# Lightning attention and a gated feed-forward on one core: k and v of two batches held with their chunks in swapped rows, and states made per chunk beside scores and outputs

## The chip, the core and the metric

The kernel runs on one core of a Trainium2 chip. A core has a matrix engine (TensorE, PE in the profile; its weight loads are PEld), a vector engine (VectorE, DVE), a scalar engine (ScalarE, ACT), GpSimd (POOL) and a sync engine (SP). They run side by side, each through its own instructions in order, and wait for each other by semaphores. Matmuls write to PSUM, which has eight banks of 128 partitions by 512 float32; all else lies in SBUF. Loads that change the type from float32 to bfloat16 are issued by GpSimd here, the others by SyncE and ScalarE.

The metric is the device time of one execution in microseconds (us). The kernel before takes 224.22 us, the median of three runs from 223.85 to 224.42.

## What is computed

q, k and v have the shape 4 batches x 8 heads x 768 positions x 64. Attention is linear, with a decay lam per head and causal in blocks of 64; its output goes through a gated feed-forward with 512 inputs, 1536 hidden units and 512 outputs.

```python
for b in range(nb):                                   # blocks of 64 positions
    qb, kb, vb = q[:, :, sl], k[:, :, sl], v[:, :, sl]
    intra = einsum('bhic,bhjc->bhij', qb, kb) * Dmask  # lam ** (i - j) for i >= j
    intra = einsum('bhij,bhjd->bhid', intra, vb)
    inter = einsum('bhid,bhde->bhie', qb * lam_pow, kv_state)
    out[:, :, sl] = intra + inter
    kv_state = lam_block * kv_state + einsum('bhsd,bhse->bhde', kb * rev_pow, vb)
x = out as (batch x position, head x 64)
gate = 1 / (1 + exp(-(x @ w_gate)))
y = (gate * (x @ w_val)) @ w_out
```

## The kernel before

It works in six steps n = 0 to 5 of 128 positions of all four batches, which is 512 rows of the feed-forward. From step 2 on, each step is two chunks c = 0, 1 of 64 positions, and position 64 c + i lies in partition row 64 c + i of the tiles of k and v. `bp` numbers the pairs of batches (0 and 1; 2 and 3).

While TensorE does the feed-forward of step n, it does the attention of step n + 1 in between. The feed-forward is 12 pieces `gv(n, ft)` (four matmuls of 128x512 for the gate `gp`, four for the value `vp`), then four `po(n, tt)` of 12 matmuls each. The list `more[ft]` is put behind piece ft. So TensorE leaves the wide matmuls three times per step, for a burst of small ones of 64x64: the scores (`chunk_s`, behind piece 4, for step 2 behind piece 5), the state products (`chunk_c`, behind piece 8) and the outputs (`chunk_i` and `chunk_a`, behind piece 11).

A matmul of 64x64 uses one quarter of the array: the half of its rows in which its two operands lie, and the half of its columns that is the half of the partitions where its output lies. The loops are laid so that four such matmuls in a row use the four quarters.

Of the eight PSUM banks five go round in `ps_at` (attention) and three in `ps_ff` (feed-forward). A tile of a pool takes the buffer that was given out longest ago, and its first matmul waits until that buffer's last reader is done.

```python
    ps_at = ctx.enter_context(tc.tile_pool(name="ps_at", bufs=5, space=bass.MemoryType.PSUM))
    ps_ff = ctx.enter_context(tc.tile_pool(name="ps_ff", bufs=3, space=bass.MemoryType.PSUM))
    # ...
    def rows_of(u):
        return slice(u * 64, (u + 1) * 64)

    def half(b, h):
        return (1 - h % 2) if b >= NB2 else h % 2

    def load(n, what, b0=0, b1=B):
        sl = slice(n * C, (n + 1) * C)
        for c in what:
            if (c, n) not in T_:
                T_[c, n] = qkv.tile([128, B, H, D], BF16, tag=c + "b", name=c + "b",
                                      bufs=5 if c == "v" else 4)
            src = {"q": q, "k": k, "v": v}[c]
            nat = b1 if n == 0 or c == "v" else min(b1, NB2)
            if b0 < nat:
                nc.gpsimd.dma_start(
                    out=T_[c, n][:, b0:nat],
                    in_=src[b0:nat, :, sl, :].rearrange("b h s d -> s (b h) d"))
            if nat < b1:
                m = max(nat, b0)
                for u in range(2):
                    nc.gpsimd.dma_start(
                        out=T_[c, n][:, m:b1, u::2, :],
                        in_=src[m:b1, 1 - u::2, sl, :].rearrange("b h s d -> s (b h) d"))
    # ...
    def chunk(c):
        return slice(c * L, (c + 1) * L)

    def chunk_s(n, bp):
        sp = [ps_at.tile([128, 2, HP, L], FP32, name=f"sp{u}", tag="ps") for u in range(2)]
        for j in range(2):
            b = 2 * bp + j
            for hp in range(HP):
                for u in range(2):
                    for c in range(2):
                        nc.tensor.matmul(sp[u][rows_of(c), j, hp, :],
                                         lhsT=KS[n, b][rows_of(u), hp, chunk(c)],
                                         rhs=QS[n, b][rows_of(u), hp, chunk(c)],
                                         start=(j == 0 and hp == 0), stop=(j == 1 and hp == HP - 1),
                                         skip_group_check=True)
        SP[n, bp] = sp

    def chunk_i(n, banks):
        name = None
        for hp in range(HP):
            for j in range(2):
                for u in range(2):
                    for c, bp in banks:
                        w, b = u ^ bp, 2 * bp + j
                        name = nc.tensor.matmul(
                            OP[n, c, bp][rows_of(w), hp, j, :], lhsT=ST[n, c][rows_of(u), bp, hp, j, :],
                            rhs=QS[n, b][rows_of(u), hp, chunk(c)],
                            start=(hp == 0 and j == 0), stop=False,
                            skip_group_check=True).ins.name
        return name

    def chunk_a(n, banks):
        name = None
        for hp in range(HP):
            for j in range(2):
                for w in range(2):
                    for c, bp in banks:
                        b, h = 2 * bp + j, 2 * hp + w
                        name = nc.tensor.matmul(
                            OP[n, c, bp][rows_of(w), hp, j, :], lhsT=T_["v", n][rows_of(c), b, h, :],
                            rhs=MT[n, bp][rows_of(c), slot(n, b, h) % 2, j, hp, :],
                            start=False, stop=(hp == HP - 1 and j == 1),
                            skip_group_check=True).ins.name
        return name

    def chunk_c(n, bp, cs=(0, 1)):
        cp = [ps_at.tile([128, HP, 2, 64], FP32, name=f"cp{c}", tag="ps") for c in cs]
        for hp in range(HP):
            for j in range(2):
                for w in range(2):
                    for c in cs:
                        b, h = 2 * bp + j, 2 * hp + w
                        nc.tensor.matmul(cp[c][rows_of(half(b, h)), hp, j, :],
                                         lhsT=KD[n][rows_of(c), b, slot(n, b, h), :],
                                         rhs=T_["v", n][rows_of(c), b, h, :],
                                         start=(hp == 0 and j == 0),
                                         stop=(hp == HP - 1 and j == 1), skip_group_check=True)
        CP[n, bp] = cp

    def update_0(n, bp):
        if bp == 0:
            new_st(n, 1)
        nc.vector.tensor_tensor(
            out=ST[n, 1][:, bp].rearrange("p h j d -> p h (j d)"), in0=XD[n][:, bp * HP:(bp + 1) * HP],
            in1=CP[n, bp][0].rearrange("p h j d -> p h (j d)"), op=ALU.add)

    def update_1(n, bp):
        if bp == 0:
            new_st(n + 1, 0)
        for hp in range(HP):
            nc.vector.scalar_tensor_tensor(
                out=ST[n + 1, 0][:, bp, hp], in0=ST[n, 1][:, bp, hp], scalar=dec_l[:, bp, hp:hp + 1],
                in1=CP[n, bp][1][:, hp], op0=ALU.mult, op1=ALU.add)
    # ...
    def piece_gv(n, ft):
        if (n, ft) not in GV:
            new_gv(n, ft)
        gp, vp = GV[n, ft]
        sg = htp.tile([128, TCH], FP32, tag="sg", name="sg", bufs=3)
        order = [(gp, WG, whole), (vp, WV, whole)]
        # ... (the halves apart in the first pieces)
        for ps, W, part in order:
            product(n, ft, ps, W, part)
            if ps is gp and part is not first:
                nc.scalar.activation(sg, gp.rearrange("p a b -> p (a b)"), AF.Tanh, scale=0.5)
        HT[n, ft] = htp.tile([128, TCH], BF16, tag="ht", name="ht", bufs=2 * NFT)
        mul = gate_value(HT[n, ft], sg, vp.rearrange("p a b -> p (a b)"))
    # ...
    A = ((0, 0), (1, 1))
    Z = ((0, 1), (1, 0))

    def att(n):
        # ... (block, for step 1)
        def chunks():
            new_xt(n)
            for c, bp in A + Z:
                new_op(n, c, bp)
            done = [chunk_i(n, banks) for banks in (A, Z)]
            for name, banks in zip(done, (A, Z)):
                in_order(name)
                chunk_a(n, banks)
                for c, bp in banks:
                    chunk_x(n, c, bp)
        return block if n < FIRST_XBAR else chunks
    # ...
    for n in range(1, NSTEP):
        nx = n + 1
        more = [[] for i in range(NFT)]
        if nx < NSTEP:
            late = 1 if n == 1 else 0
            cs = (0, 1) if nx < NSTEP - 1 else (0,)
            more[2 * late].append(do(decayed, nx))
            for bp in range(2):
                more[2 + late + bp].append(do(e_q, nx, [2 * bp, 2 * bp + 1]))
                more[4 + late].append(do(chunk_s, nx, bp))
                more[8].append(do(chunk_c, nx, bp, cs))
            for bp in range(2):
                more[4 + late + bp].append(do(chunk_m, nx, bp))
                more[8].append(do(update_0, nx, bp))
                if 1 in cs:
                    more[9 + bp].append(do(update_1, nx, bp))
            more[4].insert(0, do(make_kd, nx))
            for i in range(4):
                more[4 + i].append(kd(nx, 2 * i))
            more[11].append(att(nx))
        # ... (the loads ahead, and the stores of step 0)
        for ft in range(NFT):
            gv(n, ft, *more[ft])
        for tt in range(B):
            # ... (the last tile of the last step goes in two parts)
            more = [lambda n=n: next_loads(n + 3)] if tt == B - 1 and n + 3 < NSTEP else []
            po(n, tt, *more)
```

Of the kernel before, what the change touches and what calls it, by code (L numbers as in the profile page):

```python
# [8 lines left out]
FP32 = mybir.dt.float32  # L9
BF16 = mybir.dt.bfloat16  # L10
AF = mybir.ActivationFunctionType
ALU = mybir.AluOpType
# [4 lines left out]
def kernel(  # L17
# [11 lines left out]
    nc = tc.nc  # L29

    B, H, S, D = q.shape
    C = 128
    NSTEP = S // C
    HP = H // 2
# [5 lines left out]
    NB2 = B // 2  # L40
# [13 lines left out]
    ps_at = ctx.enter_context(tc.tile_pool(name="ps_at", bufs=5, space=bass.MemoryType.PSUM))  # L54
    ps_ff = ctx.enter_context(tc.tile_pool(name="ps_ff", bufs=3, space=bass.MemoryType.PSUM))
# [4 lines left out]
    FIRST_XBAR = 2  # L60
    L = C // 2
# [11 lines left out]
    T_ = {}  # L73

    def swapped(n, b):
        return n > 0 and b >= NB2

    def slot(n, b, h):
        return h ^ 1 if swapped(n, b) else h
# [11 lines that stand above are left out]
                T_[c, n] = qkv.tile([128, B, H, D], BF16, tag=c + "b", name=c + "b",  # L91
                                      bufs=5 if c == "v" else 4)
            src = {"q": q, "k": k, "v": v}[c]
            nat = b1 if n == 0 or c == "v" else min(b1, NB2)
            if b0 < nat:
                nc.gpsimd.dma_start(  # L96
                    out=T_[c, n][:, b0:nat],
                    in_=src[b0:nat, :, sl, :].rearrange("b h s d -> s (b h) d"))
            if nat < b1:
                m = max(nat, b0)  # L100
                for u in range(2):
                    nc.gpsimd.dma_start(  # L102
                        out=T_[c, n][:, m:b1, u::2, :],
                        in_=src[m:b1, 1 - u::2, sl, :].rearrange("b h s d -> s (b h) d"))

    def pairs(src, b0, b1):
        return src[b0:b1, :, 0:C, :].rearrange("b (r g) (p e) d -> g p b r (e d)", g=2, e=2)
# [22 lines left out]
    KD = {}  # L130
# [22 lines left out]
    ST, CP, XD = {}, {}, {}  # L153
# [117 lines left out]
    QS, KS, MT, XT, SP, OP = {}, {}, {}, {}, {}, {}  # L271
# [173 lines left out]
# [7 lines that stand above are left out]
            for hp in range(HP):  # L452
                for u in range(2):
                    for c in range(2):
                        nc.tensor.matmul(sp[u][rows_of(c), j, hp, :],  # L455
                                         lhsT=KS[n, b][rows_of(u), hp, chunk(c)],
                                         rhs=QS[n, b][rows_of(u), hp, chunk(c)],
                                         start=(j == 0 and hp == 0), stop=(j == 1 and hp == HP - 1),
                                         skip_group_check=True)
        SP[n, bp] = sp  # L460
# [25 lines left out]
# [5 lines that stand above are left out]
                    for c, bp in banks:  # L491
                        b, h = 2 * bp + j, 2 * hp + w
                        name = nc.tensor.matmul(  # L493
                            OP[n, c, bp][rows_of(w), hp, j, :], lhsT=T_["v", n][rows_of(c), b, h, :],
                            rhs=MT[n, bp][rows_of(c), slot(n, b, h) % 2, j, hp, :],
                            start=False, stop=(hp == HP - 1 and j == 1),
                            skip_group_check=True).ins.name
        return name
# [5 lines left out]
    def chunk_x(n, c, bp):  # L504
        nc.scalar.copy(XT[n][:, bp].rearrange("p m (j c i) -> p m j c i", j=2, c=2)[:, :, :, c, :],  # L505
                       OP[n, c, bp])

    def chunk_c(n, bp, cs=(0, 1)):
        cp = [ps_at.tile([128, HP, 2, 64], FP32, name=f"cp{c}", tag="ps") for c in cs]
        for hp in range(HP):  # L510
            for j in range(2):
                for w in range(2):
                    for c in cs:
                        b, h = 2 * bp + j, 2 * hp + w
                        nc.tensor.matmul(cp[c][rows_of(half(b, h)), hp, j, :],  # L515
                                         lhsT=KD[n][rows_of(c), b, slot(n, b, h), :],
                                         rhs=T_["v", n][rows_of(c), b, h, :],
                                         start=(hp == 0 and j == 0),
                                         stop=(hp == HP - 1 and j == 1), skip_group_check=True)
        CP[n, bp] = cp  # L520

    def decayed(n):
        XD[n] = stp.tile([128, 2 * HP, 2 * 64], FP32, tag="xd", name="xd", bufs=1)
# [3 lines left out]
            op=ALU.mult)  # L527

    def update_0(n, bp):
        if bp == 0:  # L530
            new_st(n, 1)
        nc.vector.tensor_tensor(
            out=ST[n, 1][:, bp].rearrange("p h j d -> p h (j d)"), in0=XD[n][:, bp * HP:(bp + 1) * HP],
            in1=CP[n, bp][0].rearrange("p h j d -> p h (j d)"), op=ALU.add)

    def update_1(n, bp):
        if bp == 0:
            new_st(n + 1, 0)
        for hp in range(HP):
            nc.vector.scalar_tensor_tensor(  # L540
                out=ST[n + 1, 0][:, bp, hp], in0=ST[n, 1][:, bp, hp], scalar=dec_l[:, bp, hp:hp + 1],
                in1=CP[n, bp][1][:, hp], op0=ALU.mult, op1=ALU.add)

# [165 lines left out]
    def do(f, *args, **kw):  # L711
        return lambda: f(*args, **kw)

    A = ((0, 0), (1, 1))
    Z = ((0, 1), (1, 0))

    def att(n):
        def block():
            piece_i(n)
            piece_a(n, range(B))  # L720
            piece_x(n, range(B))
            for bp in range(2):
                piece_c(n, bp)
# [8 lines that stand above are left out]
                chunk_a(n, banks)  # L732
                for c, bp in banks:
                    chunk_x(n, c, bp)
        return block if n < FIRST_XBAR else chunks

    def kd(n, h0, h1=None, **kw):
        return do(piece_kd, n, range(h0, h1 or h0 + 2), **kw)
# [25 lines left out]
    for n in range(1, NSTEP):  # L764
        nx = n + 1
        more = [[] for i in range(NFT)]
        if nx < NSTEP:
            late = 1 if n == 1 else 0
            cs = (0, 1) if nx < NSTEP - 1 else (0,)
            more[2 * late].append(do(decayed, nx))  # L770
            for bp in range(2):
                more[2 + late + bp].append(do(e_q, nx, [2 * bp, 2 * bp + 1]))
                more[4 + late].append(do(chunk_s, nx, bp))
                more[8].append(do(chunk_c, nx, bp, cs))
            for bp in range(2):
                more[4 + late + bp].append(do(chunk_m, nx, bp))
                more[8].append(do(update_0, nx, bp))
                if 1 in cs:
                    more[9 + bp].append(do(update_1, nx, bp))
            more[4].insert(0, do(make_kd, nx))  # L780
            for i in range(4):
                more[4 + i].append(kd(nx, 2 * i))
            more[11].append(att(nx))
        if n == 1:
            more[0].append(chunk_lamq)
            more[2].append(lambda: next_loads(2))
            more[7].append(lambda: tc.add_manual_dep(nc.sync.nop().ins, MUL[1, 7], SYNC,
                                                     reason="the loads ahead of the stores"))
            more[7].extend([lambda tt=tt, e=e: store_0(tt, e) for tt in range(B) for e in range(2)])
            more[8].append(lambda: next_loads(3))  # L790
# [3 lines that stand above are left out]
            if n == NSTEP - 1 and tt == B - 1:  # L794
                po(n, tt, c=(0, 384), eng=nc.vector)
                po(n, tt, c=(384, 512))
            else:
                more = [lambda n=n: next_loads(n + 3)] if tt == B - 1 and n + 3 < NSTEP else []
                po(n, tt, *more)
# [35 lines left out]
```

## Time and profile before

| | |
|---|---|
| time | 224.22 us (223.85 to 224.42) |
| span of the profiled execution | 222.4 us, TensorE's granted clock 1.000 |
| TensorE busy | 215.0 us, 97% of the span |
| VectorE, ScalarE, GpSimd busy | 103.9, 108.0 and 64.8 us |
| wide matmuls (128x512) of the feed-forward | 280 + 280 + 268 in the trace |
| small matmuls (64x64) of steps 2 to 5 | 256 scores, 512 outputs, 224 state products |
| loads of k, v and q issued by GpSimd per step from step 2 on | 3, 1 and 3 |

The profile gives the busy time of each engine, the chain of work that ended last (followed back from the last instruction), the groups of instructions with the idle time ahead of each and what ended it, and the loads with the time from issue to landing. The trace behind it answers with single instructions in order of time. A matmul's duration runs until its result is out, and matmuls overlap in the array; so what a stretch of TensorE costs is read here from the start of one instruction to the start of a later one, and not by adding durations.

### The profile page before, as it was taken

The page shows a single profiled execution, that of the slowest core. Times are in us where ns is not written, and L with a number is a line of the kernel's source. Part 1 is how long each engine was busy: PE and PEld are TensorE (multiplying, and loading weights), DVE is VectorE, ACT ScalarE, POOL GpSimd, SP SyncE. Part 2 cuts the span into 40 slices and gives each one's busy share as a digit, 9 for nine tenths or more (in the row PEclk, how much of TensorE's full clock was granted, in tenths as well). Part 3 has the DMA queues.
Part 4 walks back from the last instruction along what each step waited for, and adds up shares of the span by engine and source line. Part 5 has one row for each costly group of instructions (what it writes and reads, how often), then busy time and mean ns, then how long its engine had stood idle before and what let it go on. Part 6 is the DMA issues. An engine that isn't in the chain of part 4 may idle for free.

```text
span 222.4 us, 5449 instructions
## 1 busy us (share of the span) xinstructions
PE 215.0 (97%) x2300; PEld 107.5 (48%) x2310; DVE 103.9 (47%) x192; ACT 108.0 (49%) x236; POOL 64.8 (29%) x85
## 2 busy tenths in 40 slices
PE   7779999999999999999999999999999999999994
PEld 2564444557444544444544444544444544444443
DVE  4855675539687501785600785700676400333301
ACT  5748754595384523385433386342366342333221
POOL 7999855730392008501920030000000000000000
PEclk9999999999999999999999999999999999999999
DMA  6999999999999999998999894012100012100022
GB/s 116 177 179 186 196 199 182 167 156 166 134 86 159 253 200 154 180 179 122 85 158 220 205 68 31 3 50 94 47 3 0 3 50 95 47 0 1 3 94 96
DMA packets 99401, 25.27 MB, mean 114 GB/s; under 512 B 90032, under 2 KB 96432, under 8 KB 99376
## 3 DMA queue, kind: packets, MB, share of 16 engines
q0 software_dynamic: 77872, 13.90, 78.0%
q1 hardware_dynamic: 20688, 10.69, 20.0%
q10 hardware_dynamic: 816, 0.33, 0.6%
q8 instruction: 18, 0.29, 0.5%
q14 instruction: 7, 0.06, 0.1%
HBM read 28.32 MB, written 6.29 MB: 156 GB/s over the span
## 4 chain that ended last, share of the span: by engine, by line
PE 91%; POOL 4%; DMA 3%; issue 1%; ACT 0%; POOLq 0%
PE gp L555 28%; PE po L595 28%; PE vp L555 28%; DMA WV<-in_moe_w_val_dram 3%; POOL vb L114 1%; PE sp L455 1%; PE cp L515 1%; PE op L479 1%; POOL qb L114 1%; PE op L493 1%; POOL kb L114 1%; PE sp L381 0%; PE op L412 0%; PE tq L279 0%; PE tk L279 0%
## 5 line engine op out<-in xcount | busy, mean ns | idle before, releaser
L550 DVE SCALAR_TENSOR_TENSOR ht<-sg,vp 128x512 bf16<-128x512 f32 x72 | 49.4, 686 | 92.7 <-PE vp L555 87.1
L555 PE MATMUL vp<-XT,WV 128*128 128x512 bf16 (+1 forms) x296 | 74.3, 373 | 0.6 <-DMA WV<-in_moe_w_val_dram 0.6
L555 PE MATMUL gp<-XT,WG 128*128 128x512 bf16 (+1 forms) x296 | 74.3, 373 | 0.5 <-ACT XT L320 0.5
L573 ACT ACTIVATE sg<-gp 128x512 f32<-128x512 f32 x72 | 43.0, 597 | 59.2 <-PE gp L555 59.2
L595 PE MATMUL po<-WO,ht 128*128 128x512 bf16 (+2 forms) x292 | 63.3, 370 | 0.5 <-issue 0.2
L555 PEld LDWEIGHTS <-WV 128*128 128x128 bf16 x296 | 28.9, 98 | 33.9 <-DMA WV<-in_moe_w_val_dram 0.7
L595 PEld LDWEIGHTS <-ht 128*128 128x128 bf16 x300 | 28.3, 98 | 31.9
L555 PEld LDWEIGHTS <-WG 128*128 128x128 bf16 x296 | 28.3, 98 | 31.7 <-issue 0.4
L599 ACT ACTIVATE ob<-po 128x512 f32<-128x512 f32 (+1 forms) x24 | 14.0, 583 | 38.6 <-PE po L595 38.6
L143 ACT ACTIVATE kd<-kb,kds 128x128 bf16<-128x128 bf16 x80 | 25.2, 390 | 0.0
L674 POOL COPY gates<-qt 128x1 bf16<-128x1 bf16 x4 | 1.6, 388 | 49.8 <-DMA qt<-qb 49.8
L505 ACT CAST XT<-op 128x512 bf16<-128x512 f32 x16 | 8.2, 599 | 5.0 <-PE op L493 5.0
L465 DVE TENSOR_TENSOR MT<-sp,mask 128x512 bf16<-128x512 f32 x16 | 10.2, 681 | 0.0
L96 POOL DMA_DIRECT2D vb<-in_v_dram x6 | 9.0, 1501 | 3.0 <-issue 1.4
L102 POOL DMA_DIRECT2D qb<-in_q_dram x10 | 8.8, 893 | 3.1 <-DMA WO<-in_moe_w_out_dram 3.1
L102 POOL DMA_DIRECT2D kb<-in_k_dram x10 | 9.0, 919 | 1.0 <-DMA WG<-in_moe_w_gate_dram 0.5
L121 POOL DMA_DIRECT2D WV<-in_moe_w_val_dram x9 | 7.6, 856 | 0.0
L118 POOL DMA_DIRECT2D WG<-in_moe_w_gate_dram x8 | 6.8, 848 | 0.0
L540 DVE SCALAR_TENSOR_TENSOR st<-st,pow_l,cp 128x128 bf16<-128x128 bf16 x24 | 6.7, 340 | 0.0
L612 PE MATMUL zps<-st 128*128 128x512 f32 (+1 forms) x8 | 5.0, 780 | 1.5 <-DVE st L174 1.5
L96 POOL DMA_DIRECT2D kb<-in_k_dram x5 | 5.9, 1185 | 1.0 <-DMA WG<-in_moe_w_gate_dram 1.0
L96 POOL DMA_DIRECT2D qb<-in_q_dram x5 | 5.8, 1156 | 0.5 <-DMA WO<-in_moe_w_out_dram 0.5
(93 smaller groups left out, 125.7 us busy)
## 6 DMA issues: line engine op xcount, KB each, us to landing
out_dram<-ob SPq DMA_DIRECT2D x19, 256.0 KB, 2.0
vb<-in_v_dram POOLq DMA_DIRECT2D x4, 512.0 KB, 7.3
qb<-in_q_dram POOLq DMA_DIRECT2D x14, 128.0 KB, 7.6
kb<-in_k_dram POOLq DMA_DIRECT2D x12, 128.0 KB, 9.1
WO<-in_moe_w_out_dram POOLq DMA_DIRECT2D x4, 384.0 KB, 12.1
kb<-in_k_dram POOLq DMA_DIRECT2D x5, 256.0 KB, 9.2
qb<-in_q_dram POOLq DMA_DIRECT2D x5, 256.0 KB, 8.3
WG<-in_moe_w_gate_dram POOLq DMA_DIRECT2D x4, 256.0 KB, 6.8
```

The lines of the kernel that those rows point to most:

```text
L96: nc.gpsimd.dma_start(out=T_[c, n][:, b0:nat], in_=src[b0:nat, :, sl, :].rearrange("b h s d -> s (b h) d"))
L102: nc.gpsimd.dma_start(out=T_[c, n][:, m:b1, u::2, :], in_=src[m:b1, 1 - u::2, sl, :].rearrange("b h s d -> s (b h) d"))
L118: nc.gpsimd.dma_start(out=WG[:, :, f0 * 128:f1 * 128], in_=wg_r[:, :, f0 * 128:f1 * 128])
L121: nc.gpsimd.dma_start(out=WV[:, :, f0 * 128:f1 * 128], in_=wv_r[:, :, f0 * 128:f1 * 128])
L143: nc.scalar.mul(KD[n][:, at, i, :], T_["k", n][:, at, i, :], kds[:, min(n // FIRST_XBAR, 1), h:h + 1])
L465: nc.vector.tensor_tensor(out=MT[n, bp][:, u], in0=SP[n, bp][u], in1=mask[:, u ^ bp].unsqueeze(1).to_broadcast([128, 2, HP, L]), op=ALU.mult)
L505: nc.scalar.copy(XT[n][:, bp].rearrange("p m (j c i) -> p m j c i", j=2, c=2)[:, :, :, c, :], OP[n, c, bp])
L550: return nc.vector.scalar_tensor_tensor(out=o, in0=g, scalar=1.0, in1=x, op0=ALU.add, op1=ALU.mult)
L555: nc.tensor.matmul(ps[:, part], lhsT=W[:, mt, fs], rhs=XT[n][:, part, mt], start=(part is not second and mt == 0), stop=(part is not first ...
L573: nc.scalar.activation(sg, gp.rearrange("p a b -> p (a b)"), AF.Tanh, scale=0.5)
L595: nc.tensor.matmul(po[:, :c1 - c0], lhsT=HT[n, ft][:, tt * 128:(tt + 1) * 128], rhs=WO[:, ft, c0:c1], start=(ft == 0), stop=(ft == NFT - 1))
L599: (eng.mul if eng is nc.scalar else eng.tensor_scalar_mul)(o, po[:, :c1 - c0], 0.5)
```

## The change

In steps 3 to 5 the attention takes two bursts instead of three. `chunk_c` used to make the state products of both chunks of a pair of batches. Now it makes those of one chunk for all batches: chunk 0 directly behind the scores, and chunk 1 directly behind the outputs (step 5 needs no chunk 1, as no step follows). So that the products of one chunk still use all four quarters of the array, k and v of batches 2 and 3 are loaded with the two chunks in swapped rows from step 2 on: chunk c lies in rows `rows_of(c ^ bp)`. Scores, outputs and state products follow that with `c ^ bp`. The outputs now go chunk by chunk (`A` is chunk 0 of all batches, `Z` is chunk 1).

The loads of batches 2 and 3 are cut by halves of the rows for it: k of a step takes five loads instead of three, v three instead of one. The decayed keys (`piece_kd`) are made behind pieces 2 to 5 rather than 4 to 7, and scores with the first state products stand behind piece 6. One of the two tiles of each set of state products comes from `ps_ff`, the feed-forward's pool. Step 2 keeps its three bursts at their places.

```diff
# ... (some lines of context cut throughout)
--- before.py
+++ after.py
@@ -91,17 +91,22 @@
-            nat = b1 if n == 0 or c == "v" else min(b1, NB2)
+            turned = n >= FIRST_XBAR and c != "q"
+            nat = b1 if c == "v" and not turned else min(b1, NB2)
             if b0 < nat:
                 nc.gpsimd.dma_start(
                     out=T_[c, n][:, b0:nat],
                     in_=src[b0:nat, :, sl, :].rearrange("b h s d -> s (b h) d"))
             if nat < b1:
                 m = max(nat, b0)
-                for u in range(2):
-                    nc.gpsimd.dma_start(
-                        out=T_[c, n][:, m:b1, u::2, :],
-                        in_=src[m:b1, 1 - u::2, sl, :].rearrange("b h s d -> s (b h) d"))
+                for r in range(2) if turned else (None,):
+                    rows = slice(None) if r is None else rows_of(1 - r)
+                    ts = sl if r is None else slice(n * C + r * L, n * C + (r + 1) * L)
+                    for hs, hd in ((slice(0, H), slice(0, H)),) if c == "v" else (
+                            (slice(u, H, 2), slice(1 - u, H, 2)) for u in range(2)):
+                        nc.gpsimd.dma_start(
+                            out=T_[c, n][rows, m:b1, hs, :],
+                            in_=src[m:b1, hd, ts, :].rearrange("b h s d -> s (b h) d"))
 
@@ -452,8 +457,8 @@
             for hp in range(HP):
                 for u in range(2):
                     for c in range(2):
-                        nc.tensor.matmul(sp[u][rows_of(c), j, hp, :],
-                                         lhsT=KS[n, b][rows_of(u), hp, chunk(c)],
+                        nc.tensor.matmul(sp[u][rows_of(c ^ bp), j, hp, :],
+                                         lhsT=KS[n, b][rows_of(u), hp, chunk(c ^ bp)],
                                          rhs=QS[n, b][rows_of(u), hp, chunk(c)],
                                          start=(j == 0 and hp == 0), stop=(j == 1 and hp == HP - 1),
                                          skip_group_check=True)
@@ -491,8 +496,8 @@
                     for c, bp in banks:
                         b, h = 2 * bp + j, 2 * hp + w
                         name = nc.tensor.matmul(
-                            OP[n, c, bp][rows_of(w), hp, j, :], lhsT=T_["v", n][rows_of(c), b, h, :],
-                            rhs=MT[n, bp][rows_of(c), slot(n, b, h) % 2, j, hp, :],
+                            OP[n, c, bp][rows_of(w), hp, j, :], lhsT=T_["v", n][rows_of(c ^ bp), b, h, :],
+                            rhs=MT[n, bp][rows_of(c ^ bp), slot(n, b, h) % 2, j, hp, :],
                             start=False, stop=(hp == HP - 1 and j == 1),
                             skip_group_check=True).ins.name
         return name
@@ -505,19 +510,18 @@
         nc.scalar.copy(XT[n][:, bp].rearrange("p m (j c i) -> p m j c i", j=2, c=2)[:, :, :, c, :],
                        OP[n, c, bp])
 
-    def chunk_c(n, bp, cs=(0, 1)):
-        cp = [ps_at.tile([128, HP, 2, 64], FP32, name=f"cp{c}", tag="ps") for c in cs]
+    def chunk_c(n, c, pools):
+        CP[n, c] = [p.tile([128, HP, 2, 64], FP32, name=f"cp{c}", tag="ff" if p is ps_ff else "ps") for p in pools]
         for hp in range(HP):
             for j in range(2):
                 for w in range(2):
-                    for c in cs:
+                    for bp in range(2):
                         b, h = 2 * bp + j, 2 * hp + w
-                        nc.tensor.matmul(cp[c][rows_of(half(b, h)), hp, j, :],
-                                         lhsT=KD[n][rows_of(c), b, slot(n, b, h), :],
-                                         rhs=T_["v", n][rows_of(c), b, h, :],
+                        r = rows_of(c ^ bp)
+                        nc.tensor.matmul(CP[n, c][bp][rows_of(half(b, h)), hp, j, :],
+                                         lhsT=KD[n][r, b, slot(n, b, h), :], rhs=T_["v", n][r, b, h, :],
                                          start=(hp == 0 and j == 0),
                                          stop=(hp == HP - 1 and j == 1), skip_group_check=True)
-        CP[n, bp] = cp
 
     def decayed(n):
         XD[n] = stp.tile([128, 2 * HP, 2 * 64], FP32, tag="xd", name="xd", bufs=1)
@@ -527,19 +531,19 @@
             op=ALU.mult)
 
     def update_0(n, bp):
-        if bp == 0:
+        if (n, 1) not in ST:
             new_st(n, 1)
         nc.vector.tensor_tensor(
             out=ST[n, 1][:, bp].rearrange("p h j d -> p h (j d)"), in0=XD[n][:, bp * HP:(bp + 1) * HP],
-            in1=CP[n, bp][0].rearrange("p h j d -> p h (j d)"), op=ALU.add)
+            in1=CP[n, 0][bp].rearrange("p h j d -> p h (j d)"), op=ALU.add)
 
     def update_1(n, bp):
-        if bp == 0:
+        if (n + 1, 0) not in ST:
             new_st(n + 1, 0)
         for hp in range(HP):
             nc.vector.scalar_tensor_tensor(
                 out=ST[n + 1, 0][:, bp, hp], in0=ST[n, 1][:, bp, hp], scalar=dec_l[:, bp, hp:hp + 1],
-                in1=CP[n, bp][1][:, hp], op0=ALU.mult, op1=ALU.add)
+                in1=CP[n, 1][bp][:, hp], op0=ALU.mult, op1=ALU.add)
 
 
 
@@ -711,8 +715,8 @@
-    A = ((0, 0), (1, 1))
-    Z = ((0, 1), (1, 0))
+    A = ((0, 0), (0, 1))
+    Z = ((1, 0), (1, 1))
 
     def att(n):
         def block():
@@ -732,6 +736,10 @@
                 chunk_a(n, banks)
                 for c, bp in banks:
                     chunk_x(n, c, bp)
+            if FIRST_XBAR < n < NSTEP - 1:
+                chunk_c(n, 1, (ps_at, ps_ff))
+                for bp in (1, 0):
+                    update_1(n, bp)
@@ -766,20 +774,28 @@
         more = [[] for i in range(NFT)]
         if nx < NSTEP:
             late = 1 if n == 1 else 0
-            cs = (0, 1) if nx < NSTEP - 1 else (0,)
             more[2 * late].append(do(decayed, nx))
             for bp in range(2):
                 more[2 + late + bp].append(do(e_q, nx, [2 * bp, 2 * bp + 1]))
-                more[4 + late].append(do(chunk_s, nx, bp))
-                more[8].append(do(chunk_c, nx, bp, cs))
+            kd_at = 4 if n == 1 else 2
+            more[kd_at].insert(0, do(make_kd, nx))
+            for i in range(4):
+                more[kd_at + i].append(kd(nx, 2 * i))
+            at = 5 if n == 1 else 6
             for bp in range(2):
-                more[4 + late + bp].append(do(chunk_m, nx, bp))
-                more[8].append(do(update_0, nx, bp))
-                if 1 in cs:
+                more[at].append(do(chunk_s, nx, bp))
+            if n == 1:
+                for bp in range(2):
+                    more[at + bp].append(do(chunk_m, nx, bp))
+                for c in range(2):
+                    more[8].append(do(chunk_c, nx, c, (ps_at, ps_at)))
+                for bp in range(2):
+                    more[8].append(do(update_0, nx, bp))
                     more[9 + bp].append(do(update_1, nx, bp))
-            more[4].insert(0, do(make_kd, nx))
-            for i in range(4):
-                more[4 + i].append(kd(nx, 2 * i))
+            else:
+                more[at].append(do(chunk_c, nx, 0, (ps_at, ps_ff)))
+                more[at].extend([do(update_0, nx, 1), do(chunk_m, nx, 0)])
+                more[at + 1].extend([do(chunk_m, nx, 1), do(update_0, nx, 0)])
             more[11].append(att(nx))
         if n == 1:
             more[0].append(chunk_lamq)
```

## The prediction

> **What bounds the kernel now.** I read the shares of busy time first, then the chain that ended last, then what single instructions waited for.
>
> ```profile
> PE 215.0 (97%) x2300; PEld 107.5 (48%) x2310; DVE 103.9 (47%) x192; ACT 108.0 (49%) x236; POOL 64.8 (29%) x85
> PE 91%; POOL 4%; DMA 3%; issue 1%; ACT 0%; POOLq 0%
> ...
> PEld L515 <- issue: 1.7, 4, 0.4
> PEld L479 <- issue: 1.7, 4, 0.4
> PEld L455 <- issue: 1.7, 4, 0.4
> ...
> PE vp L555 <- DMA WV<-in_moe_w_val_dram: 0.6, 1, 0.6
> ```
>
> The first line is the busy time of each engine, the second the chain, the rest are waits (total, times, longest). TensorE is busy throughout, the chain is TensorE from the first feed-forward piece to the end, and its waits for other engines or loads all lie in the opening (the longest there is 1.5 us). From step 1 on only one kind of idle time stands out: 1.7 / 4 = 0.42 us of the weight loads' lane at the first instruction of each burst of small matmuls (L455 scores, L515 state products, L479 outputs). "issue" says that nothing visible was waited for. So this kernel can only gain from fewer or cheaper TensorE instructions, or from fewer changes between wide and small ones.
>
> What a burst costs is read from TensorE's timeline in steps 3, 4 and 5, always around the state products:
>
> ```profile
> 101.68 1.03 PE L555 MATMUL vp<-XT,WV 128*128 128x512 bf16 x4
> 102.64 0.74 PE L515 MATMUL cp<-vb,kd 64*64 64x64 bf16 x64
> 103.31 1.04 PE L555 MATMUL gp<-XT,WG 128*128 128x512 bf16 x4
> 104.18 1.03 PE L555 MATMUL vp<-XT,WV 128*128 128x512 bf16 x4
> ...
> 135.66 1.03 PE L555 MATMUL vp<-XT,WV 128*128 128x512 bf16 x4
> 136.62 0.73 PE L515 MATMUL cp<-vb,kd 64*64 64x64 bf16 x64
> 137.29 1.04 PE L555 MATMUL gp<-XT,WG 128*128 128x512 bf16 x4
> ...
> 169.65 1.03 PE L555 MATMUL vp<-XT,WV 128*128 128x512 bf16 x4
> 170.60 0.69 PE L515 MATMUL cp<-vb,kd 64*64 64x64 bf16 x32
> 171.22 1.04 PE L555 MATMUL gp<-XT,WG 128*128 128x512 bf16 x4
> 172.10 1.03 PE L555 MATMUL vp<-XT,WV 128*128 128x512 bf16 x4
> ```
>
> The columns are start, duration, engine and form. Four wide matmuls follow the next four after 0.864 us (0.86 all along the chain). In step 3, 103.31 - 101.68 - 0.864 = 0.77 us lie in between, in step 4 the same, in step 5 0.71, and there the next piece adds 0.88 - 0.864 = 0.02, so 0.72. What 64 more small matmuls cost inside a burst is seen where two sets follow each other without a change:
>
> ```profile
> 142.57 0.71 PE L479 MATMUL op<-QS,st 64*64 64x64 bf16 x64
> 143.10 0.79 PE L493 MATMUL op<-MT,vb 64*64 64x64 bf16 x64
> ```
>
> 143.10 - 142.57 = 0.53 us, or 8.3 ns each. So a burst of 64 has 0.77 - 0.53 = 0.24 us of fixed cost, 0.10 of it ahead (last wide start 102.33 to first small start 102.64 is 0.31, where 0.216 is the pace) and 0.14 behind. The burst of step 5 has half as many matmuls and costs almost as much: 0.72 - 0.24 = 0.48 us for 32, 15 ns each. The code tells why: with `cs = (0,)` all 32 read rows 0 to 63, so only two quarters of the array take turns.
>
> [...]
>
> **The change part by part.** *Removed:* one burst per step in steps 3, 4 and 5. Steps 3 and 4 lose the fixed cost: the 64 state products remain, 32 in the scores' burst, 32 in the outputs' burst, at 32 x 8.3 = 0.27 us each, if four quarters are used. They are: with w = 0 the pair bp 0 uses rows c and columns 0, bp 1 the other rows and columns 1, and w = 1 takes the other two. So -0.24 us each. *Step 5:* its 0.72 us go and 0.27 come back: -0.45 us. Sum on TensorE's path: 0.24 + 0.24 + 0.45 = 0.93 us. Scores and outputs keep count and quarters (row half `c ^ bp` where it was `c`).
>
> *Moved on ScalarE:* the decayed keys stand behind pieces 2 to 5. A tanh starts 0.49 us ahead of them and a set of four takes 1.24 us up to the next tanh (134.14 - 132.91 = 1.23), together 1.73 us for a piece of 1.728. They just fit, as they do today in pieces 5 to 7, and TensorE needs that tanh only a piece later. No cost.
>
> *Moved on VectorE:* behind the new burst stand `update_0` of pair 1, two mask products, then behind the next piece two more and `update_0` of pair 0. Next instructions start 0.60 us apart in all three (137.40 follows 136.80 by 0.60; two mask products take 1.20 in 132.22 to 133.42). With T the start of piece 7: the first update can begin at about T + 0.1, the mask products at 0.7, `ht` of piece 7 when its matmuls are done at about 2.0 (last start 1.53 + the 0.48 between 131.14 and 131.62), mask products at 2.6, update at 3.8, `ht` of piece 8 at 4.4, done at 5.1. In the pool of three banks the extra tile takes one turn, so the gate of piece 10 gets the bank that `ht` 8 reads. It starts at T + 3 x 1.728 + 0.02 = 5.2. The margin is 0.1 us less the semaphore's way. I put the cost at 0.02 us on average per step, 0.05 in all. The third tile in the outputs' burst is read by `update_1` directly behind, about 2.5 us before the third `po` needs its bank: nothing.
>
> *Added on GpSimd:* per step two k loads and two v loads, 16 in all. 4096 rows of 64 values take 1.68 us to issue (v), 2048 take 1.18, 1024 take 0.91; by that line 512 take an estimated 0.77. So k goes from 3.0 to 4.3 us and v from 1.68 to 3.0, about 10 us more over four steps on an engine that is busy for 64.8 of 222. Rows and bytes are the same. Only step 2 is tight. Its v is issued here and landed 7.1 us after the start, at 67.8, and its products start at 68.64:
>
> ```profile
> 60.13 0.62 POOL L674 COPY gates<-kt 128x1 bf16<-128x1 bf16 x1 [0.58 <-DMA kt<-kb]
> 60.69 1.68 POOL L96 DMA_DIRECT2D vb<-in_v_dram  x1
> 62.35 1.16 POOL L96 DMA_DIRECT2D qb<-in_q_dram  x1
> ```
>
> 0.8 us of room. With v in three loads the first half leaves 0.5 us earlier and the last quarter 1.3 later; 512 KB pass in about 3.2 us here (the next 256 KB land 1.65 us later), so the last quarter should find the queue still busy. The transposed k of step 2 is there at 60.1 and needed at 62.68. Its loads queue for 9 us before they land, so 1.3 us more of issuing should not delay them. No cost expected, one chance in eight of a stall of 0.3 to 1 us. The later steps' loads lead their use by 10 us and more.
>
> Sum: -0.93 + 0.05 = about -0.9 us; 224.22 - 0.9 = 223.3 us.
>
> **The rivals.** (1) *The array does not take the merged set at full rate*, because the row halves alternate from one matmul to the next: 32 products at 15 ns would be 0.48 us in each of five places instead of 0.27, +1.05 us, and the gain is gone: 224.3. Against it: today's outputs alternate rows in the same manner and run at 8.3 ns. (2) *A new wait takes the place of the fixed cost*: TensorE waiting for `ht` 8 at piece 10. For it speaks the thin margin, and one `ht` in step 4 that started at 129.50 where its matmuls were due at 129.11. At 0.2 us in each of three steps, 223.9. (3) *The loads of step 2 come late*: 223.6 to 224.3. (4) *Only the fixed cost goes*, step 5 keeping its half rate: 223.5.
>
> **Range and chances.** The three runs before span 0.57 us, so the median moves by some 0.3 either way. Rival 1 or 3 in full would bring it to 224.3, no gain; I see nothing that brings more than 1.1 us. I choose 222.8 to 224.0. 2% is 4.5 us, five times what the change touches.
>
> **What would show it.** Two sets of `issue` idle time per step in steps 3 to 5; 1.04 us (0.77 + 0.27) between the wide matmuls around the scores' burst, 1.34 + 0.27 = 1.61 us around the outputs' burst; 120 to 154 (one step) 0.24 us shorter than today's 33.98; step 5's state products at 8.3 ns; no wait of `gp` for `ht`; products of step 2 without a wait for v. The prediction is wrong if TensorE shows new idle time behind piece 9, if the first products of step 2 wait for a load, or if the merged burst takes over 1.2 us.

## The result, and the profile after

The changed kernel takes 223.66 us (median; 223.28 to 223.73) against 224.30 us; the ratio is 0.9971, with a 95% interval from 0.9958 to 0.9983. Two repeats, each beside new runs of the kernel before, gave 223.57 us (0.9968; 0.9955 to 0.9980) and 223.47 us (0.9963; 0.9950 to 0.9976). So the gain is 0.6 to 0.9 us. It was forecast at 0.9.

The page after shows the same bound. First the shares of busy time and the chain by engine, then the three rows of waits in which the weight loads' lane stood idle at the start of a burst (total, times, longest):

```profile
PE 216.0 (98%) x2310; PEld 107.4 (48%) x2310; DVE 104.5 (47%) x192; ACT 107.8 (49%) x236; POOL 72.9 (33%) x101
PE 92%; POOL 4%; DMA 3%; issue 0%; ACT 0%; POOLq 0%
...
PEld L460 <- issue: 1.7, 4, 0.4
PEld L484 <- issue: 1.7, 4, 0.4
...
PEld L521 <- issue: 0.4, 1, 0.4
```

Scores and outputs still open a burst four times each. The state products (now L521) open one once instead of four times, in step 2; in steps 3 to 5, where they follow other small matmuls, no such wait stands ahead of them. GpSimd is busy 8.1 us longer, and TensorE does not wait for it.

TensorE's timeline of the changed kernel, the two bursts of step 3 (start, duration, engine and form):

```profile
97.47 1.03 PE L559 MATMUL vp<-XT,WV 128*128 128x512 bf16 x4
98.43 0.71 PE L460 MATMUL sp<-QS,kt 64*64 64x64 bf16 x64
98.96 0.45 PE L521 MATMUL cp<-vb,kd 64*64 64x64 bf16 x32
99.34 1.04 PE L559 MATMUL gp<-XT,WG 128*128 128x512 bf16 x4
...
107.12 1.03 PE L559 MATMUL vp<-XT,WV 128*128 128x512 bf16 x4
108.08 0.71 PE L484 MATMUL op<-QS,st 64*64 64x64 bf16 x64
108.61 0.79 PE L498 MATMUL op<-MT,vb 64*64 64x64 bf16 x64
109.22 0.50 PE L521 MATMUL cp<-vb,kd 64*64 64x64 bf16 x32
109.65 2.55 PE L599 MATMUL po<-WO,ht 128*128 128x512 bf16 x11
```

Between the wide matmuls lie 99.34 - 97.47 - 0.864 = 1.01 us, and 109.65 - 107.12 - 0.864 = 1.67 us.

The most useful measure is the time from the first gate matmul of one feed-forward step to that of the next. It leaves out the opening, whose length wanders from run to run (the first gate of step 1 starts anywhere from 52.1 to 52.6 us in these profiles). Each interval contains one attention step. All kernels of this study, from one profile each:

| kernel | with step 2 | step 3 | step 4 | step 5 | ratio to before (95% interval) |
|---|---|---|---|---|---|
| before | 34.02 | 33.99 | 33.97 | 33.94 | |
| changed | 34.00 | 33.77 | 33.77 | 33.45 | 0.9971 (0.9958 to 0.9983) |
| x_three | 33.99 | 33.98 | 33.99 | 33.69 | 0.9987 (0.9981 to 0.9994) |
| x_four | 34.00 | 34.33 | 34.18 | 33.69 | 1.0006 (1.0000 to 1.0013) |
| x_noswap | 34.37 | 34.19 | 34.19 | 33.67 | 1.0022 (1.0012 to 1.0033) |
| x_masks | 34.00 | 34.01 | 33.91 | 33.58 | 0.9983 (0.9973 to 0.9992) |
| x_cfirst | 33.99 | 33.91 | 33.75 | 33.45 | 0.9962 (0.9949 to 0.9974) |
| x_step2 | 33.93 | 33.77 | 33.77 | 33.45 | 0.9959 (0.9947 to 0.9972) |
| x_step2b | 33.93 | 33.94 | 33.77 | 33.45 | 0.9959 (0.9945 to 0.9972) |
| x_both | 34.46 | 33.91 | 33.74 | 33.45 | 0.9965 (0.9951 to 0.9978) |

The change gives 0.22 + 0.20 + 0.49 = 0.91 us over steps 3 to 5, and the two repeats show its four intervals again within 0.01 us.

### The profile page after: what moved, and what is told of

The parts are those of the page before. It is cut to its first block, busy times and chain, and to the rows that moved or that the text cites. A ratio compares the mean times of both kernels' runs of the same rounds, so it can differ in the third digit from the quotient of the medians.

```text
span 221.5 us, 5489 instructions
## 1 busy us (share of the span) xinstructions
PE 216.0 (98%) x2310; PEld 107.4 (48%) x2310; DVE 104.5 (47%) x192; ACT 107.8 (49%) x236; POOL 72.9 (33%) x101
## 4 chain that ended last, share of the span: by engine, by line
PE 92%; POOL 4%; DMA 3%; issue 0%; ACT 0%; POOLq 0%
PE po L599 28%; PE gp L559 28%; PE vp L559 28%; DMA WV<-in_moe_w_val_dram 3%; POOL vb L119 1%; PE sp L460 1%; PE op L484 1%; POOL qb L119 1%; PE op L498 1%; PE cp L521 1%; POOL kb L119 1%; PE sp L386 0%; PE op L417 0%; PE tk L284 0%; PE tq L284 0%
## 5 line engine op out<-in xcount | busy, mean ns | idle before, releaser
L107 POOL DMA_DIRECT2D kb<-in_k_dram x18 | 12.9, 763 | 2.7 <-DMA vb<-in_v_dram 1.7
L107 POOL DMA_DIRECT2D qb<-in_q_dram x10 | 8.9, 903 | 2.9 <-DMA WO<-in_moe_w_out_dram 2.9
L97 POOL DMA_DIRECT2D vb<-in_v_dram x6 | 6.9, 1152 | 2.7 <-issue 1.1
L616 PE MATMUL zps<-st 128*128 128x512 bf16 (+1 forms) x10 | 6.2, 748 | 1.5 <-DVE st L179 1.5
L107 POOL DMA_DIRECT2D vb<-in_v_dram x8 | 6.6, 831 | 0.0
L97 POOL DMA_DIRECT2D kb<-in_k_dram x5 | 6.0, 1192 | 1.1 <-DMA WG<-in_moe_w_gate_dram 1.1
```

Of the source, the lines that this page charges most:

```text
L97: nc.gpsimd.dma_start(out=T_[c, n][:, b0:nat], in_=src[b0:nat, :, sl, :].rearrange("b h s d -> s (b h) d"))
L107: nc.gpsimd.dma_start(out=T_[c, n][rows, m:b1, hs, :], in_=src[m:b1, hd, ts, :].rearrange("b h s d -> s (b h) d"))
```

## The experiments

**How many bursts.** The theory is a fixed cost per burst and, in step 5, the quarters of the array. The main rival is that the split loads cost something that the medians hide. Three kernels have the new layout and the new loads and differ in the number of bursts: two (the changed kernel), three, and four.

`x_again`, the yardstick, is the changed kernel unedited:

> The changed kernel once more, as the yardstick for the other runs. Theory (a fixed cost per burst goes, and step 5's state products get four quarters): 0.6 to 0.9 us below the kernel before, feed-forward steps of 33.77, 33.77 and 33.45 us between first gates as in the first profile.

`x_three` goes back to the places of before:

```diff
-            if FIRST_XBAR < n < NSTEP - 1:      # in att(n), behind the outputs
-                chunk_c(n, 1, (ps_at, ps_ff))
-                for bp in (1, 0):
-                    update_1(n, bp)
-            kd_at = 4 if n == 1 else 2
-            at = 5 if n == 1 else 6
+            kd_at, at = 4, 4 + late
+            for bp in range(2):
+                more[at + bp].append(do(chunk_m, nx, bp))
+            for c in (0, 1) if nx < NSTEP - 1 else (0,):
+                more[8].append(do(chunk_c, nx, c, (ps_at, ps_at)))
+            # update_0 and update_1 behind pieces 8 to 10, as before
```

> The changed layout with its split loads, but three bursts per step at the places of before. Theory: only step 5's products gain (0.72 us to about 0.51 around them), steps 3 and 4 take 33.98 us as before; 0.2 us below before, 0.7 above the changed kernel. Rival 'split loads cost something': at or above the time of before. Rival 'the layout itself brings the gain': as fast as the changed kernel.

It took 224.09 us against 223.57 for `x_again`, 0.52 more (0.66 by the intervals, where 0.7 was expected). Steps 3 and 4 are back at 33.98 and 33.99, and only step 5 gained: 33.69, which is 0.25 less than before. Its burst in `x_three`:

```profile
169.62 1.03 PE L559 MATMUL vp<-XT,WV 128*128 128x512 bf16 x4
170.57 0.45 PE L521 MATMUL cp<-vb,kd 64*64 64x64 bf16 x32
170.95 1.04 PE L559 MATMUL gp<-XT,WG 128*128 128x512 bf16 x4
```

170.95 - 169.62 - 0.864 = 0.47 us for 32 products where the kernel before needs 0.71. So of the 0.49 us of step 5, 0.25 come from the swapped rows and 0.24 from the burst. The loads cost nothing in any interval, and the split-load rival falls.

`x_four` parts the sets of products from scores and outputs. The second set stands alone between two output products of the feed-forward:

```diff
+                more[8].append(do(chunk_c, nx, 0, (ps_at, ps_at)))
+                # update_0 behind it; the mask products as in the kernel before
+                if tt == 0 and 1 < n < NSTEP - 2:
+                    more.append(do(chunk_c, n + 1, 1, (ps_at, ps_at)))
+                    more.extend([do(update_1, n + 1, bp) for bp in range(2)])
                 po(n, tt, *more)
```

> Four bursts per step in steps 3 and 4 and three in step 5: each set of 32 state products alone, the last between two output products of the feed-forward. Theory: each lone set costs 0.27 us plus a fixed 0.22 to 0.24, so five bursts more than in the changed kernel: 1.1 to 1.2 us above it, about 0.3 us above before. Rival 'the place behind the scores and the outputs, not the number of bursts, brings it': less than 0.5 us above the changed kernel.

It took 224.56 us, 0.99 above the yardstick; by intervals 0.56 + 0.41 + 0.24 = 1.21. Step 4, two bursts more than in the changed kernel, costs 0.41, or 0.20 each; step 5, one more, costs 0.24. In step 3, about 0.16 of the 0.56 are a standstill in the midst of the scores (0.83 us to the next wide matmul, where step 4 has 0.67), of which more below. The rival (the place brings it, less than 0.5 us) falls. Two, three and four bursts in step 4 take 33.77, 33.99 and 34.18 us: about 0.2 us for each.

**What the swapped rows are worth.** `x_noswap` keeps two bursts, but loads k and v as the kernel before does; `c ^ bp` becomes `c` everywhere, and the outputs go in the old order:

```diff
-            turned = n >= FIRST_XBAR and c != "q"
+            turned = False
+            # nat as in the kernel before
-                        r = rows_of(c ^ bp)                    # and so in chunk_s and chunk_a
+                        r = rows_of(c)
-    A = ((0, 0), (0, 1))
-    Z = ((1, 0), (1, 1))
+    A = ((0, 0), (1, 1))
+    Z = ((0, 1), (1, 0))
```

> Two bursts as in the changed kernel, but k and v with their chunks in natural rows and the loads of before, so that each set of 32 state products reads one half of the rows. Theory (one row half: 15 ns a matmul against 8.3): seven sets in steps 2 to 5 at 0.48 us instead of 0.27, 1.5 us above the changed kernel, 0.8 above before. Rival 'the quarters do not matter, the bursts do': as fast as the changed kernel.

224.99 us, 1.42 above the yardstick and slower than the kernel before. The intervals give 0.37 + 0.42 + 0.42 + 0.22 = 1.43. The burst of scores and first products in step 4 of `x_noswap`:

```profile
133.31 0.71 PE L460 MATMUL sp<-QS,kt 64*64 64x64 bf16 x64
133.84 0.67 PE L521 MATMUL cp<-vb,kd 64*64 64x64 bf16 x32
134.44 1.04 PE L559 MATMUL gp<-XT,WG 128*128 128x512 bf16 x4
```

From the first product to the next wide matmul pass 0.60 us; in the changed kernel it is 99.34 - 98.96 = 0.38. Less the tail of 0.11 that a full set leaves (0.38 - 32 x 8.3 ns), 32 products from one half of the rows take 0.49 us, 15 ns each. Merging the bursts without the swap thus costs more than it saves, and the change has no gain without the swapped rows.

Why one half of the rows is slower is not shown. The products of `x_noswap` use one half of the rows and so only two quarters. So do the 32 products of step 5 in the kernel before, and their single starts in the trace come in pairs 3 to 4 ns apart, mostly with 28 to 29 ns to the next pair. The state products of step 3 there, which use four quarters, start mostly in fours, 3 to 4 ns apart, with about 22 ns to the next four. By an estimate from these starts a quarter takes one product every 32 ns or so in both. Two quarters in different row halves were not tried, so it stays open whether the row half or the number of quarters, to which the prediction put it down, sets the pace.

**VectorE's order behind the merged burst.** The prediction saw a margin of 0.1 us at the gate of piece 10. `x_masks` takes the margin away by putting all four mask products and the second update ahead of the product of piece 7:

```diff
-                more[at].extend([do(update_0, nx, 1), do(chunk_m, nx, 0)])
-                more[at + 1].extend([do(chunk_m, nx, 1), do(update_0, nx, 0)])
+                more[at].extend([do(update_0, nx, 1), do(chunk_m, nx, 0), do(chunk_m, nx, 1), do(update_0, nx, 0)])
```

> The changed kernel with one thing moved on VectorE: all four mask products and the second state update stand behind piece 6, ahead of the product of piece 7, which so ends 4.6 us after the burst instead of 2.7. Theory (the third bank lent to the state products makes the gate of piece 9 wait for that product): 1.1 us of TensorE idle in each of steps 3 to 5, about 3.4 us above the changed kernel, 227.0. Rival 'VectorE has slack there and its order does not matter': the time of the changed kernel.

It took 224.02 us where 227.0 was expected, and the intervals lost 0.24, 0.14 and 0.13 us: a wait, so the rival (no wait at all) falls too, but with 0.51 us in all about a seventh of the 3.4 expected. VectorE and TensorE in step 3:

```profile
102.95 0.68 DVE L536 TENSOR_TENSOR st<-xd,cp 128x512 bf16<-128x512 f32 x1
103.54 1.28 DVE L554 SCALAR_TENSOR_TENSOR ht<-sg,vp 128x512 bf16<-128x512 f32 x2
...
102.30 1.03 PE L559 MATMUL vp<-XT,WV 128*128 128x512 bf16 x4
103.17 1.03 PE L559 MATMUL gp<-XT,WG 128*128 128x512 bf16 x4
104.28 1.02 PE L559 MATMUL vp<-XT,WV 128*128 128x512 bf16 x4
```

The product of piece 7 runs from 103.54 to about 104.2. The gate of piece 9 starts at 103.17, before that product has begun, so it does not wait for it. The value of piece 9 starts at 104.28, where 103.17 + 0.864 = 104.03 was its turn. So the bank of piece 7's value went not to the gate of piece 9, as I had it for this experiment, but by these times to the value behind it, 0.864 us later. The description of the pools ahead of the prediction (a tile takes the bank given out longest ago) does not hold here; by which rule the pool hands out banks, these runs do not show. In the changed kernel itself the product of piece 8 ran from 103.79 to 104.47 and the gate of piece 10 started on time at 104.53, 0.864 after the matmuls ahead of it; whether it needed that bank at all, this profile does not say.

**The outputs' burst.** It came out 0.06 us longer than worked out. `x_cfirst` puts the second products between the two halves of the outputs:

```diff
             done = [chunk_i(n, banks) for banks in (A, Z)]
+            if FIRST_XBAR < n < NSTEP - 1:      # moved up from the end of att(n)
+                chunk_c(n, 1, (ps_at, ps_ff))
+                for bp in (1, 0):
+                    update_1(n, bp)
```

> The changed kernel with the second state products ahead of the output products with v instead of behind them. In the changed kernel that burst takes 1.67 us where 1.61 was worked out; 0.08 of it passes between the 64 output products with v and the state products. Theory (the output products with v are held back by the order kept against the ones with the state): the lag goes, 0.05 to 0.1 us less in each of steps 3 and 4, too little for the median. Rival 'the products with v are slower in themselves': step times of 33.77 as in the changed kernel.

Step 4 took 33.75 us instead of 33.77 (step 3 has a standstill in its scores, 0.67 us to the next set where step 4 has 0.54, and is not compared). In step 4 of `x_cfirst`:

```profile
142.64 0.46 PE L521 MATMUL cp<-vb,kd 64*64 64x64 bf16 x32
142.93 0.78 PE L498 MATMUL op<-MT,vb 64*64 64x64 bf16 x64
143.65 2.55 PE L599 MATMUL po<-WO,ht 128*128 128x512 bf16 x10
```

The 64 output products with v take 0.72 us to the next wide matmul, or 0.61 less a tail of 0.11. In the changed kernel it is 109.22 - 108.61 = 0.61 too, so the lag that I had seen ahead of the state products is no lag: this set is slower in itself, 9.5 ns a matmul on average instead of 8.3, wherever it stands, and it was so in the kernel before (143.82 - 143.10 = 0.72). The theory falls, for the step gained 0.02 us and not 0.05 to 0.1. What was longer than worked out is the 32 state products behind it: 109.65 - 109.22 = 0.43 us where behind the scores it is 0.38. Single starts show that neither set has a slower pace throughout: most products follow each other by 8 to 9 ns, and the excess lies in a few gaps of 16 to 34 ns. The output products with v have them at the start, around the place where the second half `Z` begins, and at the last two products; the state products behind the outputs have them at the start and the end. What makes these gaps was not tried.

**Step 2 as well.** `x_step2` gives step 2 the two bursts that steps 3 to 5 have, with its scores moved behind piece 8:

```diff
-            at = 5 if n == 1 else 6
+            at = 8 if n == 1 else 6
-            if n == 1:
-                ...                              # the three bursts of step 2
-            else:
+            # the two bursts for every step
-            if FIRST_XBAR < n < NSTEP - 1:
+            if n < NSTEP - 1:
```

> The changed kernel with step 2 in two bursts as well: its scores and first state products behind piece 8, its second state products behind the outputs. Theory (0.21 to 0.24 us per burst taken away): 0.2 us below the changed kernel, the first of the four feed-forward steps 33.78 instead of 34.00 us. Rival 'no room behind piece 8': the outputs behind piece 11 wait for the masks or for the state of chunk 1, and the step takes 34.0 us or more.

223.51 us. The interval with step 2 fell by 0.07 us instead of 0.22, as the burst stood still for 0.12 us in the midst of its state products:

```profile
68.71 0.59 PE L521 MATMUL cp<-vb,kd 64*64 64x64 bf16 x32
69.24 1.04 PE L559 MATMUL gp<-XT,WG 128*128 128x512 bf16 x4
```

The 32 products take 69.24 - 68.71 = 0.53 us to the next wide matmul instead of 0.38. The same kernel again, with the changed kernel beside it:

> Step 2 in two bursts as well, once more and beside the changed kernel on one chip. In its first profile the first feed-forward step took 33.93 us, since its burst stood still for 0.12 us in the middle. Theory (that standstill is a chance of the run): the step takes 33.78 to 33.82 us now, and the median lies 0.1 to 0.2 us under the changed kernel. Rival (it comes from the place behind piece 8): 33.93 us again.

> The changed kernel, as the yardstick of this call. Theory: 0.6 to 0.9 us below before, feed-forward steps of 33.99, 33.77, 33.77 and 33.45 us.

223.49 us beside 223.47. The standstill came back (0.54 us from the first product to the next wide matmul), so in step 2 it is not a chance of one run, and both profiles give 33.93. A second one, again with 0.54 us, showed in step 3, where the first profile of the same kernel has none (33.94 against 33.77 us), so that one does differ between executions of one kernel. No gain over the changed kernel is shown.

`x_both` joins `x_step2` and `x_cfirst`:

> Both of the foregoing: step 2 in two bursts, and the second state products ahead of the output products with v, in steps 2 to 4. Theory: the sum, 0.2 to 0.5 us below the changed kernel, 223.2. Rival: no faster than the changed kernel, if either brings a wait.

223.51 us, no faster than the changed kernel (223.47 to 223.66). Step 2's outputs' burst, where the products now stand in the middle, shows the largest standstill of the study:

```profile
75.07 0.34 PE L521 MATMUL cp<-vb,kd 64*64 64x64 bf16 x18
75.81 0.31 PE L521 MATMUL cp<-vb,kd 64*64 64x64 bf16 x14 [0.40 <-issue]
75.93 0.75 PE L498 MATMUL op<-MT,vb 64*64 64x64 bf16 x64
```

18 of the 32 products are out, and the next follows about 0.6 us later, with nothing in the profile that it waited for ("issue"). The interval is 34.46 us. The profiled execution took 224.12 us and the other four 223.38 to 223.63, so this largest one does not show in the median and may be a chance of that execution.

## Why the prediction was right

**The bound and the fixed cost** held. TensorE stayed the bound, and each burst taken away from steps 3 and 4 gave 0.22 and 0.20 us, where the prediction had 0.24; the runs show this cost and not what makes it. Its split into terms was off in two places that partly cancel: the scores' burst took 1.01 us (1.04 forecast), the outputs' burst 1.67 (1.61 forecast). The mis-sized term is the 32 state products behind the outputs, which add 0.33 us to that burst instead of 0.27.

**Step 5** gave 0.49 us where 0.45 was forecast, and `x_three` parts it into 0.25 for the swapped rows and 0.24 for the burst. The 15 ns of one row half came back in `x_noswap`. That the sum (0.91 us by the intervals, 0.88 forecast) came out so close is in part luck: steps 3 and 4 gave 0.06 less than forecast, step 5 gave 0.04 more, and the 0.05 set aside for VectorE did not come.

**Loads.** GpSimd rose by 8.1 us (about 10 forecast): four quarter loads of k took 2.76 to 2.80 us to issue, not 4 x 0.77, and two of the v loads 1.64 to 1.65, not 2 x 0.91. Two of the quarter loads of step 2's k waited for older loads of v, 0.99 and 0.72 us, which the prediction did not foresee. It cost nothing: step 2's interval is 34.00 in the changed kernel. Its v loads landed 4.3 to 4.6 us after issue, so by about 67.3 us, and their products began at 68.67 without a wait.

**ScalarE** just fitted, as worked out: from piece 2's decayed keys to the tanh of piece 6 one instruction follows the other without a gap (91.26 to 97.67 us in step 2 of the feed-forward), and no TensorE wait came of it.

**VectorE's margin** is the step that failed, though it cost nothing. The prediction booked 0.05 us for it, and named the gate of piece 10 as the one that waits. No such wait shows in the changed kernel. Where `x_masks` makes one, it falls on another tile and is about a seventh of what the same reasoning gave for that run, since the order in which the pool hands out banks was assumed and not read.

**The rivals.** Rival 1 (half rate) did not come, and `x_noswap` shows its size: 1.43 us over seven sets, so about 1.0 in the five places named. The argument against it held, but pointed at the wrong set: the outputs that run at 8.3 ns (`chunk_i`) change the row half at every second matmul, and those that change it at every matmul (`chunk_a`) took 9.5. The set that shows it is the state products of the kernel before, which change the row half at every matmul and start 8.3 ns apart on average. Rival 2 came only where it was made. Rivals 3 and 4 are ruled out by the intervals with steps 2 and 5. The measured medians lie between 0.6 and 0.9 us below the kernel before while the intervals give 0.91. In the profiles, what lies behind the last of these intervals takes 34.3 us in both kernels, so a difference can only come from the opening, whose length wanders by 0.5 us; for the medians that is not shown.

## What to carry to other kernels

When the matrix engine is busy throughout, count how often it changes between forms of matmuls, and read one change's cost from the starts of the instructions around it: here 0.2 us a time, though in the profile of the kernel before TensorE's own waits name none of these bursts and the weight loads' lane stood idle for 0.4 us at each. Before small matmuls are merged into another burst, see that the operands' placement keeps all parts of the array in turn: here the merger without it was 0.2% slower than the kernel before (ratio 1.0022), and the placement is decided at the load. Experiments whose effect is smaller than the spread of the runs are better judged by intervals inside the trace than by medians.

## What was not expected of the hardware

Small matmuls came to a standstill in the midst of a burst in some kernels and not in others. From the first start of the set to what follows it, the scores of step 3 took 0.13 to 0.16 us longer in `x_four`, `x_cfirst` and `x_both` than those of step 4, state products took 0.53 to 0.54 us instead of 0.38 in `x_step2`, `x_step2b` and `x_both`, and once two products in `x_both` lie about 0.6 us apart. The three profiles of the changed kernel show none (their intervals agree within 0.01 us). The same kernel can show one in one execution and not in another, as step 3 of `x_step2` (33.77 us) and `x_step2b` (33.94 us) does. The trace names no releaser, and the cause stays open; no run here tells it.
